# Odd-tile stores ahead of a K halo, two weight loads later, and residual accumulates moved into the next group's MLP1

## The chip, the cores and the metric

The kernel runs on one core of one Trainium2 chip. The metric is device time in microseconds (us), the median of several executions. In the text PE is TensorE (PEld its weight loads), DVE is VectorE, ACT is ScalarE, POOL is GpSimd and SP is SyncE, whose only work here is to issue DMAs.

## The reference

Input x is 2048 tokens of 576 numbers (bf16). Two blocks follow each other.

```python
xn = layernorm(x)
q, k, v = (xn @ wqkv)                    # 32 heads of 18
idx = pos - 2 * arange(8)                # token s looks at s, s-2, ..., s-14
attn = softmax(where(idx >= 0, q . k[idx] * 18**-0.5, -1e9))
h = x + (sum_w attn[w] * v[idx[w]]) @ wo
y = layernorm(layernorm(h))
out = h + gelu(y @ w1 + b1) @ w2 + b2    # w1: 576 x 4608, w2: 4608 x 576
```

## The kernel before, in words

**Tiles.** Token s = 16 p + j sits in partition p of tile j, so there are 16 tiles of 128 tokens. A token's eight neighbours are in the same partition of the tiles j, j-2, ..., and, where that runs below tile 0, in the partition above of a tile 16 higher. So K and V are kept in two rings (`kv_ring`, one of the even and one of the odd tiles), and when attention goes on from tile j to tile j-2, slot j is overwritten by its copy shifted by one partition. This is the **halo** (line 336 on): tile j's K and V are stored to DRAM (`store_halo`, L298) and read back one row lower (`kv_ring<-kv_dram`, L339), K (`halo(j, 1)`) and V (`halo(j, 2)`) by themselves. `halo(j, t)` can only be issued once DVE has read the slot for tile j, and the next tile's DVE work waits for its landing.

**Stages.** The first stage, QKV, has 24 visits of PE, each of two products (one of q, k or v of a tile). Even tiles come first and are transposed on PE. The odd tiles' normalised x goes through DRAM: ACT writes it (`ln1_act`), `out_x(i)` stores two tiles (L284 and L285, `xd<-q_all`), and `in_x(i)` reads them back transposed (L288, `xnT<-xd`). PE uses the first pair of odd tiles from visit 12 on. The lists `after` (what follows a visit) and `loads` (weight loads after a visit) order all that by hand. `load_w1(c)` reads one of six pieces of w1, and it waits for ACT's last evacuation before it.

Then there are eight **groups** of two tiles (GROUPS, counted from 0, even tiles first, both falling). For each group PE runs MLP1 (four visits, `pm`, L217), the output projection of the next group's two tiles (`pw<-wo_sb,oT`, L217) and MLP2 (`po`; L576 in groups 0 and 1; L664 from group 2 on, where seven products do the work of eight and DVE forms their sums, L634 and L644). A visit's second phase on PE waits for a marker, a no-operation on POOL that waits for the first phase (L227). Beside PE's work on group k:

- DVE finishes the attention of group k+1 in MLP1: for its first tile the weighted sum of V (L394, L400, L401), then the same for its second tile, which needs the V halo of the first; then the logits of group k+2 (L342 to L362).
- Each attention output is stored (`td<-q_all`, L193 and L194) and read back transposed (`oT<-td`, L430) for the output projection.
- Within MLP2, `ln2_h` (L458) adds the projection to x, giving h in float32; ACT computes the two layer norms, POOL the power -0.5 (L478); SP stores the result, and `ln2_in` (L493) reads it back transposed as `hnT`, the input of the next MLP1.
- **The residual.** `put_b2` (L502) overwrites the x tile with b2, and `accumulate_h` (L504 on) adds h to it by an accumulating DMA issued from POOL (`x_all<-h`, L505), behind the transposes of `ln2_in`. MLP2 of the next group reads the sum (L695).

`ln2_ins` (L873) issues the two transposes, and for all groups but the third and the last the two accumulates straight behind them, so in the MLP2 of the group before. The third group's (GROUPS[2]) are issued by L1018 ahead of visit 1 of its own MLP1. The last group takes another way (`add_b2`) and has no accumulate.

All engines' instructions are issued in the order in which the program calls them:

```python
ins = nc.gpsimd.dma_start(out=x_of(j), in_=h_of.pop(j)[:], accum_op=ALU.add).ins
tc.add_manual_dep(ins, read[0].name, sync_dep, reason="behind the transposes of LN2")
```

Of the kernel before, what the change touches and what calls it, by code (L numbers as in the profile page):

```python
# [17 lines left out]
def kernel(  # L18
# [37 lines left out]
    GROUPS = [ATT_ORDER[i:i + 2] for i in range(0, NT, 2)]  # L56
# [435 lines left out]
    def ln2_in(j):  # L492
        read[0] = nc.sync.dma_start_transpose(out=hnT_slot(j), in_=hn.pop(j)[:]).ins  # L493
        if stored[0] is not None:
            tc.add_manual_dep(read[0], stored[0].name, sync_dep, reason="stores ahead of the transposes of LN2")
            stored[0] = None
# [179 lines left out]
    def c_(fn, *a):  # L676
        return lambda: fn(*a)
# [69 lines left out]
    def call(fns):  # L747
        for fn in fns:
            fn()

    with tc.manual_schedule(engines={ENG.PE, ENG.Activation, ENG.DVE, ENG.SP, ENG.Pool}):
# [97 lines left out]
        A = ATT_ORDER  # L849
# [23 lines left out]
        def ln2_ins(c, d):  # L873
            for j in (c, d):
                ln2_in(j)
            if c not in (GROUPS[2][0], GROUPS[-1][0]):
                accumulate_hs(c, d)

        def accumulate_hs(*js):
            for j in js:  # L880
                accumulate_h(j)

        def ln2_pair(c, d):
            ln2_stats(c, d)
            ln2_send(c)
            ln2_send(d)
            ln2_ins(c, d)

        loads = {v: [c_(load_w1, c)] for c, v in enumerate((3, 4, 9, 13, 15, 17))}
        for n, v in enumerate((19, 20, 21, 22)):  # L890
            loads[v] = loads.get(v, []) + [c_(load_w2, n)]
        after = {
# [3 lines left out]
            3: [c_(ln1_even_rstd, 6, 7), c_(ln1_stats, 8)],  # L896
            4: [c_(ln1_rstd, 8), c_(ln1_stats, 9), c_(ln1_stats, 10, c_(ln1_bias, 8))],
            5: [c_(ln1_act, 8, 0), c_(ln1_rstd, 9), c_(ln1_bias, 9), c_(att_qk_a, A[0])],
            6: [c_(ln1_rstd, 10), c_(ln1_act, 8, 1), c_(halo, A[0], 1), c_(out_x, 0)],
            7: [c_(att_qk_rest, A[0], 0), c_(ln1_bias, 10), c_(ln1_act, 8, 2)],  # L900
            8: [c_(att_qk_a, A[1]), c_(att_qk_rest, A[1], 1), c_(ln1_act, 8, 3), c_(in_x, 0), c_(out_x, 1)],
            9: [c_(halo, A[1], 1), c_(ln1_act, 9, 0)],
# [49 lines left out]
        def mlp1_plan(p, q, r, s, end):  # L952
            return [[([2 * v + n], tag) for n, tag in enumerate(tags)] for v, tags in enumerate(((p, q), (r, s), (p, q), end))]

        def mlp1(grp, plan, ahead, between, late=None):
            for v, duos in enumerate(plan):
                call(ahead.get(v, ()))
                visit([mlp1_duo(grp, us, tag) for us, tag in duos], None, between.get(v, ()), late if v == 3 else None)

        def mlp2_tile(grp, i, tag, inserts):  # L960
            po_of[grp[i]] = psum_pair(tag, "po")
            mlp2(grp, i, [po_of[grp[i]][:, half, 0:HALF] for half in range(2)], inserts)
# [11 lines left out]
        def wo_visit(*duos, fill=False):  # L974
            visit([wo_duo(j, tag) for j, tag in duos], (lambda: [ahead[0]() for _ in range(2)]) if fill else None)
# [5 lines left out]
        for k, g in enumerate(GROUPS):  # L981
            c, d = GROUPS[k + 1] if k + 1 < len(GROUPS) else (None, None)
            e, f = GROUPS[k + 2] if k + 2 < len(GROUPS) else (None, None)
            m1, mid, ia, ib, late_wo = {0: []}, {}, {}, {}, None
            if k in (1, 2):
                m1[0].append(c_(finish_out, GROUPS[k - 1][1]))
            if k == 0:
                m1[0] += [c_(halos, 1), c_(load_w2, 4), c_(att_qk_a, d), c_(att_qk_rest, d, 1), c_(halo, d, 1)]
                mid[0] = {1: [c_(exps, d)]}
                m1[1] = [c_(pv_t, c), c_(pv_t, d), c_(att_qk_a, e), c_(halo, e, 1)]  # L990
                late_wo = wo_duo(c, "B")
                ia[0] = [c_(ln2_h, c), c_(ln2_act, c), c_(put_b2, c), c_(ln2_send, c), c_(att_qk_rest, e, 0)]
                ia[19] = [lambda d=d: wo_visit((d, "A"), fill=True), c_(ln2_h, d), c_(ln2_act, d), c_(put_b2, d), c_(att_qk_a, f),
                          c_(halos, 2), c_(halo, f, 1), c_(ln2_send, d), c_(ln2_ins, c, d), c_(att_qk_rest, f, 1), c_(exps, e, f)]
                ib[0] = [c_(finish_out, g[0]), c_(att_den, e, f), c_(pv_sum, e), c_(send_o, e)]
                ib[8] = [c_(read_o, e)]
            elif k == 1:
                m1[0] += [c_(pv_sum, d), c_(send_o, d)]
                m1[1] = [c_(att_qk_a, e), c_(halo, e, 1), c_(read_o, d), c_(att_qk_b, e, 0), c_(halos, 7)]
                m1[3] = [c_(att_qk_a, f), c_(halo, f, 1), c_(att_qk_add, f, ((0, 0, 9), (0, 0, 4)))]  # L1000
                ia[0] = [c_(wo_visit, (c, "B"), (d, "C")), c_(ln2_pair, c, d), c_(att_qk_b, f, 1, 2), c_(att_max, (e, f)),
                         c_(exps, e, f), c_(w2_sums, 0, 8, (0, 1)), c_(w2_sums, 8, 12, (0, 1)), c_(att_den, e, f)]
                ia[2] = [c_(pv_sum, e), c_(dma_tr_o, e), c_(reload_x, GROUPS[4])]
                ib[0] = [c_(finish_out, g[0])]
            if k < 2:
                mlp1(g, mlp1_plan(p, q, r, s, (s, r, p) if k else (r, s, p)), m1, mid, late_wo)
                mlp2_tile(g, 0, "D", ia)
                mlp2_tile(g, 1, "C", ib)
                continue
            rows = ROWS[k]  # L1010
            x = {n: [] for n in ("hc", "h", "6", "7", "in", "exp", "4", "3")}
            if 2 < k < 7:
                m1[0] += [c_(pv_sum, c), c_(send_o, c), c_(pv_sum, d), c_(read_o, c), c_(send_o, d), c_(read_o, d)]
            if k < 6:
                m1[1], m1[3] = [c_(att_qk_one, e, 0)], []
                if k == 2:
                    m1[0] += [c_(pv_sum, d), c_(send_o, d), c_(read_o, d)]
                    m1[1] = [c_(accumulate_hs, *g)] + m1[1]  # L1018
                    m1[3] += [c_(w2_sums, 0, 8, (2, 3)), c_(w2_sums, 8, 12, (2, 3)), c_(w2_sums, 12, 14, (0, 1)), c_(w2_sums, 14, 16, (0, 1)),
                              c_(att_qk_a, f), c_(halo, f, 1)]  # L1020
                early = {2: (), 5: (0,)}.get(k, (0, 2))
                m1[3] += [c_(h_sums, 0, min(rows, SR), early)]
                if k == 5:
                    x["h"] += [c_(h_sums, 0, SR, (2,)), c_(h_sums, 0, SR, (1, 3))]
                else:
                    x["h"] += [c_(h_sums, 0, rows, [t for t in range(4) if t not in early])]
                if k == 5:
                    x["h"] += [c_(h_sums, SR, rows), c_(w2_sums, 12, 14, (2, 3)), c_(w2_sums, 14, 16, (2, 3))]
                x["7"] += [c_(att_qk_one, f, 1) if k > 2 else c_(att_qk_b, f, 1), c_(att_max, (e, f))]
                x["exp"] += [c_(exps, e, f)]  # L1030
                x["4"] += [c_(att_den, e, f)]
            else:
                if k == 6:
                    ring1_free[0] = True
                    m1[1] = [c_(w2_sums, 16, NM)]
                m1[3] = [c_(h_sums, 0, SR)]
                if k == 7:
                    mid[3] = {1: [c_(h_sums, SR, 16)]}
                    x["h"] += [c_(h_sums, 16, NM)]
            if k + 3 < len(GROUPS):  # L1040
                x["in"] += [c_(reload_x, GROUPS[k + 3])]
            wo = None
            if c is not None:
                if k == 6:
                    x["hc"] += [c_(ln2_h, c), c_(ln2_act, c)]
                    x["h"] += [c_(ln2_h, d), c_(ln2_more, d), c_(ln2_rstd, d), c_(h_sums, SR, NM), c_(ln2_send, c),
                               c_(ln2_bias, d), c_(add_b2, c), c_(add_b2, d)]
                    x["6"] += [c_(ln2_hn, d), c_(ln2_out, d)]
                else:
                    x["hc"] = [c_(ln2_h, c), c_(ln2_act, c)] + x["hc"]  # L1050
                    x["h"] = [c_(ln2_h, d), c_(ln2_act, d), c_(put_b2, c), c_(put_b2, d)] + x["h"]
                    x["6"] += [c_(ln2_send, c)]
                    x["7"] = [c_(ln2_send, d)] + x["7"]
                x["in"] = [c_(ln2_ins, c, d)] + x["in"]
                wo = lambda tags: wo_visit((c, tags[0]), (d, tags[1]))
            mlp1(g, mlp1_plan(p, q, r, s, (r, s, p)), m1, mid)
            if 3 <= k < 7:
                mlp2_fast(g, rows, (s, p, q, r), wo, x, True)
                p, q, r, s = q, r, p, s
            else:  # L1060
                mlp2_fast(g, rows, (q, p, r, s), wo, x)
                p, q, r, s = r, s, p, q
# [30 lines left out]
```

## Time and profile before

| what | value |
|---|---|
| median of 5 runs | 363.87 us (363.86 to 364.19) |
| the profiled execution | 363.96 us |
| its span | 362.2 us |
| QKV and what precedes it | to 68.66 us |
| MLP1 of groups 0 to 7 starts at (us) | 68.66, 106.73, 144.47, 180.97, 217.28, 253.55, 289.52, 325.47 |
| one MLP1 on PE | 17.79 us |
| TensorE clock granted, mean | 0.998 |

The span is from the first to the last instruction of the program; the execution is longer by what lies around it. The starts of MLP1 come from the chain of waits, which goes back from the last instruction to whatever released it. "+2.97" in the text below is 2.97 us after the MLP1 of the group in question began. A number in square brackets in a timeline is the idle time of the engine before that instruction, and the name behind it is what ended it. The time "to landing" of a DMA runs from its issue on SP or POOL to the semaphore that tells of its arrival.

### The profile page before, as it was taken

Reading aid. Unit: us, or ns where it says so; the run is one execution under the profiler, and the core shown is the slowest. Engines: PE = TensorE matmul, PEld = TensorE weight load, DVE = VectorE, ACT = ScalarE, POOL = GpSimd, SP = SyncE. Lnnn points to the kernel's source line nnn. Section 1 sums busy time; section 2 is a strip of 40 time slices with the busy share of each in tenths; the row PEclk is TensorE's granted clock in tenths of the full one; section 3 lists DMA queues with packets and bytes.
Section 4 is the critical chain, followed back from the end, with each engine's and each line's share of the span. In section 5 each row is a group of like instructions: output and inputs, shape, how many; then the busy total and the mean of one; then the engine's idle time right before and its main releaser. Section 6 shows DMA issues by size and latency. Waiting matters only on the chain.

```text
span 362.2 us, 11410 instructions
## 1 busy us (share of the span) xinstructions
PE 357.4 (99%) x4891; PEld 291.3 (80%) x4891; DVE 302.1 (83%) x422; ACT 229.4 (63%) x507; POOL 37.1 (10%) x47
## 2 busy tenths in 40 slices
PE   8999999999999999999999999999999999999996
PEld 4688977888778877887788778877887788778874
DVE  5899999999999998999899989998899999720441
ACT  4779846798636782568556945695569366705630
POOL 2241004000120020101010210020101100100000
PEclk9999999999999999999999999999999999999999
DMA  8989899964446732621443144513541442120001
GB/s 232 317 213 283 226 253 235 355 239 74 149 88 110 193 139 71 131 61 51 120 89 90 50 123 85 91 49 88 120 78 60 60 84 74 39 54 19 2 2 33
DMA packets 61907, 43.70 MB, mean 121 GB/s; under 512 B 31888, under 2 KB 60176, under 8 KB 61856
## 3 DMA queue, kind: packets, MB, share of 16 engines
q1 hardware_dynamic: 59968, 41.13, 42.9%
q0 software_dynamic: 1728, 1.77, 4.6%
q8 instruction: 38, 0.62, 0.7%
q10 hardware_dynamic: 160, 0.07, 0.1%
q14 instruction: 13, 0.11, 0.1%
HBM read 21.10 MB, written 12.42 MB: 93 GB/s over the span
## 4 chain that ended last, share of the span: by engine, by line
PE 96%; DMA 2%; SPq 1%; issue 0%; DVE 0%
PE pm L217 39%; PE po L664 27%; PE pq L217 14%; PE po L576 10%; PE pw L217 5%; DMA wq_sb<-in_A_wqkv_dram 1%; SPq L104 1%; DMA oT<-td 1%; PE xt_pt L182 1%; PE o_pt L182 0%; PE h_pt L182 0%; PE xt_pt L186 0%; DVE o_sb L695 0%; PE o_pt L186 0%; PE h_pt L186 0%
## 5 line engine op out<-in xcount | busy, mean ns | idle before, releaser
L557 ACT ACTIVATE h_all<-pm,b_sb 128x256 f16<-128x256 f32 (+1 forms) x288 | 108.5, 497 | 69.6 <-PE pm L217 69.6
L217 PE MATMUL pm<-hnT,w_sb 64*128 64x256 bf16 x2304 | 143.0, 269 | 0.0
L217 PEld LDWEIGHTS <-w_sb 64*128 64x128 bf16 x2304 | 111.7, 94 | 15.1 <-issue 1.7
L664 PEld LDWEIGHTS <-h_all 128*128 128x128 f16 x512 | 49.4, 98 | 14.2 <-issue 1.6
L217 PE MATMUL pq<-wq_sb,xnT 64*128 64x288 bf16 x768 | 54.5, 283 | 0.3 <-DMA wq_sb<-in_A_wqkv_dram 0.3
L217 PEld LDWEIGHTS <-xnT 64*128 64x128 bf16 x864 | 42.7, 94 | 10.2 <-issue 0.5
L348 DVE TENSOR_TENSOR prod<-prod 128x2304 bf16<-128x2304 bf16 (+1 forms) x64 | 44.2, 691 | 2.0
L394 DVE TENSOR_TENSOR prod<-kv_ring,probs 128x4608 bf16<-128x4608 bf16 x16 | 40.9, 2555 | 2.4 <-DMA kv_ring<-kv_dram 2.2
L342 DVE TENSOR_TENSOR prod<-kv_ring,q_all 128x4608 bf16<-128x4608 bf16 x16 | 40.8, 2550 | 0.2
L217 PE MATMUL pm<-hnT,w1h_sb 64*128 64x256 bf16 x288 | 39.2, 269 | 0.0
L664 PE MATMUL po<-w2a_sb,h_all 128*128 128x288 bf16 (+1 forms) x282 | 38.9, 286 | 0.0
L400 DVE TENSOR_TENSOR prod<-prod 128x2304 bf16<-128x2304 bf16 (+1 forms) x32 | 33.9, 1058 | 1.1
L576 PEld LDWEIGHTS <-h_all 128*128 128x128 bf16 x288 | 27.9, 98 | 7.9 <-issue 1.0
L664 PEld LDWEIGHTS <-kv_ring 128*128 128x128 f16 x252 | 24.6, 98 | 6.3
L478 POOL TENSOR_TENSOR ln_rstd<-ln_var,mhalf 128x1 f32<-128x1 f32 x13 | 12.0, 924 | 170.1 <-ACT ln_var L477 170.1
L576 PE MATMUL po<-w2a_sb,h_all 128*128 128x288 bf16 x224 | 28.5, 286 | 0.0
L664 PE MATMUL po<-w2b_sb,h_all 128*128 128x288 bf16 (+1 forms) x142 | 21.3, 286 | 0.0
L217 PE MATMUL pw<-wo_sb,oT 64*128 64x288 bf16 x256 | 19.6, 283 | 0.2 <-DMA oT<-td 0.2
L735 ACT COPY po<-po 128x288 f32<-128x288 f32 x18 | 6.9, 384 | 19.6 <-PE po L664 18.5
L644 DVE TENSOR_TENSOR kv_ring<-h_all 128x1536 f16<-128x1536 f16 (+3 forms) x9 | 6.8, 752 | 14.7 <-ACT h_all L557 14.7
L162 POOL TENSOR_TENSOR ln_rstd<-ln_veps,mhalf 128x1 f32<-128x1 f32 (+2 forms) x14 | 13.4, 967 | 48.1 <-DVE ln_veps L156 32.9
L217 PEld LDWEIGHTS <-oT 64*128 64x128 bf16 x288 | 13.7, 94 | 4.6 <-issue 0.7
(110 smaller groups left out, 388.1 us busy)
## 6 DMA issues: line engine op xcount, KB each, us to landing
w_sb<-in_B_w_dram SPq DMA_DIRECT2D x6, 768.0 KB, 6.1
kv_ring<-kv_dram SPq DMA_DIRECT2D x28, 144.0 KB, 2.7
w2a_sb<-in_B_w_dram SPq DMA_DIRECT2D x4, 1008.0 KB, 6.6
kv_dram<-kv_ring SPq DMA_DIRECT2D x13, 288.0 KB, 3.0
out_dram<-o_sb SPq DMA_DIRECT2D x15, 144.0 KB, 2.6
td<-q_all SPq DMA_DIRECT2D x14, 144.0 KB, 1.8
td<-hn SPq DMA_DIRECT2D x14, 144.0 KB, 1.8
x_all<-in_A_x_dram SPq DMA_DIRECT2D x12, 144.0 KB, 2.8
```

Of the source, the lines that this page charges most:

```text
L162: nc.gpsimd.tensor_tensor(out=rstd[:], in0=veps[:], in1=mhalf[:].to_broadcast([P, n]), op=ALU.pow)
L217: last = nc.tensor.matmul(duo["g"][r ^ swap][i], lhsT=lhsT, rhs=rhs, start=(swap == 0 and i == 0 and kt == 0), stop=(swap == 1 and kt == K ...
L342: nc.vector.tensor_tensor(out=prod[:], in0=k_ring[j % 2], in1=q_all[:, j, :].unsqueeze(1) .to_broadcast([P, W, D]), op=ALU.mult)
L348: nc.vector.tensor_tensor(out=prod[:, :, o * H:o * H + n], in0=prod[:, :, a * H:a * H + n], in1=prod[:, :, c * H:c * H + n], op=ALU.add)
L394: nc.vector.tensor_tensor(out=prod[:].rearrange("p w (d h) -> p w d h", h=H), in0=v_ring[j % 2].rearrange("p w (d h) -> p w d h", h=H), in ...
L400: nc.vector.tensor_tensor(out=prod[:, 0:n, :], in0=prod[:, 0:n, :], in1=prod[:, n:2 * n, :], op=ALU.add)
L478: nc.gpsimd.tensor_tensor(out=rstd[:], in0=var[:], in1=mhalf[:], op=ALU.pow)
L557: pace[0] = nc.scalar.activation(out=hT(grp)[:, f, 0:N], in_=ps[:, r, i * N:(i + 1) * N], func=ACT.Gelu_apprx_tanh, bias=b1_sb[:, f:f + 1] ...
L576: nc.tensor.matmul(banks[half], lhsT=hT(grp)[:, f, i * P:(i + 1) * P], rhs=w2_rows(f)[:, half * HALF:(half + 1) * HALF], start=(f == 0), s ...
L644: nc.vector.tensor_tensor(out=s_slot(t, m0, m1), in0=a, in1=b, op=alu)
L664: nc.tensor.matmul(bank, lhsT=l, rhs=r, start=start, stop=stop, skip_group_check=True)
L735: nc.scalar.copy(out=bank[seed[step][1]], in_=bank[seed[step][0]])
```

## The change

There are three parts. `accumulate_hs` of GROUPS[3] to GROUPS[6] is no longer called in `ln2_ins` but ahead of visit 1 of the group's own MLP1, where GROUPS[2] has it already; GROUPS[1] stays as it was. After visit 6 of QKV the first store of odd tiles, `out_x(0)`, is issued ahead of the first K halo. The second piece of w1 is loaded after visit 8 instead of visit 4, and the third after visit 11 instead of visit 9.

```diff
         def ln2_ins(c, d):
             for j in (c, d):
                 ln2_in(j)
-            if c not in (GROUPS[2][0], GROUPS[-1][0]):
+            if c == GROUPS[1][0]:
                 accumulate_hs(c, d)
...
-        loads = {v: [c_(load_w1, c)] for c, v in enumerate((3, 4, 9, 13, 15, 17))}
+        loads = {v: [c_(load_w1, c)] for c, v in enumerate((3, 8, 11, 13, 15, 17))}
...
-            6: [c_(ln1_rstd, 10), c_(ln1_act, 8, 1), c_(halo, A[0], 1), c_(out_x, 0)],
+            6: [c_(ln1_rstd, 10), c_(ln1_act, 8, 1), c_(out_x, 0), c_(halo, A[0], 1)],
...
                 if k == 2:
                     m1[0] += [c_(pv_sum, d), c_(send_o, d), c_(read_o, d)]
-                    m1[1] = [c_(accumulate_hs, *g)] + m1[1]
...
+            if k < 7:
+                m1[1] = [c_(accumulate_hs, *g)] + m1[1]
             mlp1(g, mlp1_plan(p, q, r, s, (r, s, p)), m1, mid)
```

## The prediction

> **What bounds the kernel now.** I read the page first. Its first lines say that TensorE (PE) is busy for nearly the whole span, and the chain that ended last is 96% PE:
>
> ```profile
> span 362.2 us, 11410 instructions
> ...
> PE 357.4 (99%) x4891; PEld 291.3 (80%) x4891; DVE 302.1 (83%) x422; ACT 229.4 (63%) x507; POOL 37.1 (10%) x47
> ...
> PE 96%; DMA 2%; SPq 1%; issue 0%; DVE 0%
> ```
>
> The change adds and removes no matmul, so it can only move the places where PE waits. I looked for them twice: in the list of waits, and by the distance between the starts of neighbouring matmuls in the trace, less the usual distance of their kind (0.055 us in MLP1, 0.061 in QKV, 0.123 in MLP2). After the first 10 us only four distances are too long without being a change of stage: 0.17 us at 36.97 (two matmuls), 0.08 at 199.24, 0.17 at 275.33 and 0.46 at 307.64. Together **0.88 us**. The list of waits names their causes (PE and PEld rows describe the same stops, from two sides):
>
> ```profile
> DVE prod L394 <- DMA kv_ring<-kv_dram: 2.2, 3, 1.6
> ...
> PEld L217 <- DMA oT<-td: 0.7, 2, 0.5
> ...
> PEld L664 <- DVE h_all L644: 0.3, 1, 0.3
> ...
> PEld L217 <- DMA xnT<-xd: 0.2, 1, 0.2
> ```
>
> So 0.88 us is the most that can be won, 0.24% of the time: the transpose of the odd tiles (36.97), the attention output of group 4's second tile (199.24), a sum of h (275.33), and the attention output of group 7's second tile (307.64). A wait of DVE, 1.6 us, stands behind the last two.
>
> **Part 1, the accumulates of groups 3 to 6** (GROUPS counted from 0; group 7 has none). They leave four places and enter four. POOL's timeline shows the old places, and at 147.44 group 2's pair, which has the new place already:
>
> ```profile
> 147.44 1.79 POOL L505 DMA_DIRECT2D x_all<-h  x2 [13.62 <-PE pm L217]
> ...
> 180.22 1.78 POOL L505 DMA_DIRECT2D x_all<-h  x2 [9.09 <-DMA x_all<-in_A_x_dram]
> ...
> 215.90 1.78 POOL L505 DMA_DIRECT2D x_all<-h  x2 [8.19 <-DMA x_all<-in_A_x_dram]
> ...
> 253.58 1.78 POOL L505 DMA_DIRECT2D x_all<-h  x2 [9.59 <-DMA x_all<-in_A_x_dram]
> ...
> 288.48 1.78 POOL L505 DMA_DIRECT2D x_all<-h  x2 [9.18 <-DVE logits L362]
> ```
>
> Group 2's MLP1 starts at 144.47 (chain of waits), so the new place is +2.97 us into the MLP1; groups 3 to 6 start at 180.97, 217.28, 253.55 and 289.52, so their pairs go to about 183.9, 220.3, 256.5 and 292.5. Three things follow.
>
> POOL: behind the pair in the queue stand the markers of visit 1, which release PE's second phases. In group 2 the pair ends at +4.76, the next marker comes at +5.17 and PE has no gap. Cost 0, with 0.4 us of cover; the pair takes 1.78 to 1.79 us in all five rows above. Here a rule speaks against the change. The Trainium skill, "SBUF — State Buffer", section "SBUF: two separate sides", warns that a VectorE instruction in a two-port mode keeps GpSimd from writing DMA descriptors, 620 ns becoming 3100. By an estimate from these figures, five times 1.79 us would end the pair at +11.9 and hold PE 6.7 us in each of four groups, 27 us in all. The row at 147.44 ran beside the same L394 multiply that the new places meet and shows none of it; I go by the row.
>
> The old places: no PE wait is released by an accumulate there. What they delay is the V halo of the next group's first tile (L339), which DVE needs for the second weighted sum (L394):
>
> ```profile
> 187.15 2.56 DVE L394 TENSOR_TENSOR prod<-kv_ring,probs 128x4608 bf16<-128x4608 bf16 x1 [0.24 <-DMA kv_ring<-kv_dram]
> ...
> 261.06 2.56 DVE L394 TENSOR_TENSOR prod<-kv_ring,probs 128x4608 bf16<-128x4608 bf16 x1 [1.58 <-DMA kv_ring<-kv_dram]
> ```
>
> The halo is issued at +3.29 in groups 3, 4 and 5, as PE's end of the group before releases it, and lands 2.8, 2.3 and 4.1 us later. In group 4 the accumulates were nearly done, 2.3 us, no wait; in group 5 they had started only at 253.58. DVE is free for L394 at +5.94, so a halo has 2.65 us.
>
> The new places: all five pairs show their first packet 1.46 to 1.47 us after their start, so at +4.43. An undisturbed halo shows its first 0.94 us after its issue, +4.23, and lands at +5.5. It is ahead by 0.2 us. **Value taken: no wait of DVE in groups 3 to 5.** The other bound: one accumulate goes first; its packets take 1.4 us on each engine (255.0 to 256.4), so the halo lands at +6.9 and DVE waits 1.0 us. I take the first as group 4's row is nearest. The packets show stretches of one queue alone (255.0 to 256.4 POOL's, 256.1 to 257.0 SP's). The skill's "DMA: Bandwidth & Descriptors", section "Queues, rings and completion order", says that a DMA engine changes queues only between packets, drained whole; by it a halo ahead by 0.2 us loses nothing, one behind loses a whole share.
>
> What the freed DVE time is worth: in group 3 the attention output landed at 199.19, for a PE that wanted it at about 199.16; 0.24 us earlier removes the stop, **-0.08**. Group 4 has 1.6 us of slack (landing 233.93, use 235.54): 0. In group 5 the next thing late is not DVE: L458 waits for PE's output projection. It ran at 273.31, +19.76; in group 4, waiting for PE, at +19.54. So 1.58 us shrink to 0.22 there. From L458 on DVE has no gap until group 7's output is done (303.25), and its store and transpose (L193, L430) land at 308.12. All that comes 0.22 us earlier: the stop at 275.33 goes, the one at 307.64 stays, and the sum of both is **-0.22**.
>
> Group 6 is the doubtful one. DVE starts its sums there 2.5 us later than in the other groups (292.75, +3.23 against +0.71), so the halo goes out at 295.1, not before the accumulates but among them: pair at 292.5, first packet 293.95, last at +4.6 to +5.1 in the quiet rows, 297.1 to 297.6. It landed in 2.05 us before; DVE leaves it 2.68. An instruction fetch of 16 KB also takes one DMA engine from 294.64 for 1.15 us. Bounds: -0 and +0.95 us (that engine does the fetch, its share of 1.4 us until 297.9, then the halo, 298.75 landed). I take 0, near the landing of 2.8 us in group 3 with both kinds of traffic, and keep +0.95.
>
> **Part 2, out_x ahead of the K halo.** SP's timeline:
>
> ```profile
> 27.93 0.34 SPq L339 DMA_DIRECT2D kv_ring<-kv_dram  x1
> 28.36 0.39 SPq L284 DMA_DIRECT2D xd<-q_all  x1
> 28.80 1.55 SPq L285 DMA_DIRECT2D xd<-q_all  x1
> 30.44 1.96 SPq L298 DMA_DIRECT2D kv_dram<-kv_ring  x4
> 32.50 1.49 SPq L288 DMA_TRANSPOSE xnT<-xd  x1
> ```
>
> ACT ends the tile for out_x at 27.91 and DVE frees the halo's slot at 27.91 too, so out_x wins 0.4 us and the halo loses 0.9, or 2.4 if it is then the one that stays 1.5 us in the queue (a fetch runs from 28.88 to 29.96, and L285 sat through it). The halo landed at 31.33; DVE wants it at 32.33. So DVE loses 0 to 1.4 us. It has 1.2 us of cover: DVE's output ends at 46.20 and PE transposes it at 47.38. Value 0, worst 0.2. The gain: the transpose L288 landed at 37.09 for a PE that wanted it at 36.95. The stores L298 between set its issue; with out_x earlier it may come 0.4 us earlier or not at all. Bounds -0.17 and 0; I take **-0.1**.
>
> **Part 3, two w1 pieces later** (768 KB each, about 6 us to landing). They go from 23.34 to about 35.2 and from 35.74 to about 41.3, and are needed in MLP1 from 68.7 on: no wait. On SP's queue they now stand before the K halo of tile 12 (needed at 54.7) and before the V halo of tile 14 (landed 46.81, needed 47.59). The latter may come up to 1 us late, 0.2 after its slack; same cover. The second transpose landed at 42.83, use about 44.0: 1.1 us of slack, and one piece in flight beside it as before. Cost 0, worst +0.3.
>
> **Sum** against the profiled execution, 363.96 us (span 362.2 and 1.8 around it): -0.08 - 0.22 - 0.1 = -0.4, so 363.56. The median of the runs shown is 363.87, 0.09 lower, so about **363.5**.
>
> **Rivals.**
> Nothing lands where PE stands: group 5's halo is as late as before (its fetch at 258.72 still falls on it) and L288 does not move. 363.7 to 364.0, about 363.85. For it: DVE's 1.58 us are worth only 0.22. Against: group 4's quiet row.
> Group 6 alone collides: -0.08 - 0.22 - 0.1 + 0.95 = +0.55, 364.4.
> **Slower**: the accumulates win the DMA engines from the V halo. Place: L394's wait in the MLP1 of groups 3 and 6, where the attention output has no slack. Price: group 3 waits 1.0 instead of 0.24, +0.76; group 6 +0.95; less 0.1 at the start: +1.6, 365.5. It decides as soon as the pair's first packet comes before the halo's, 0.2 us from now. For it: the transpose in group 2 issued 0.8 us behind the pair took 4.8 us, against 2.9 elsewhere.
> Faster: all four stops go, also the oT of group 7, if its halo and transposes meet less traffic: -0.88, 363.0. Against: DVE's unbroken run from L458 on.
>
> **How the numbers follow.** Forecast (363.3 to 363.7) 0.38; nothing 0.22; group 6 alone 0.15; slower rival, 364.6 to 365.5, 0.13; faster rival 0.12. Keeping 8 in 10 leaves out the outer half of the slower rival and little else: 363.05 to 364.9. 0.2% is 0.73 us, about what a measurement of this kernel can tell from no change. Below 363.14 only the faster rival lies: 0.12. Above 364.6 the slower one: 0.13. The rest 0.75.
>
> **What would show it.** Right: L505 pairs at +2.97 of groups 2 to 6; L394 without a wait in groups 3 to 5; L458 of group 5 at +19.54 after a PE wait; a stop of about 0.4 us before group 7's oT; no xnT wait. Wrong: L394 waits of 0.5 us or more in group 3 or 6, a PE wait for oT near 199 or above 0.6 us near 308, or a PE wait for POOL's markers in visit 1, which I price at nothing.

## The result, and the profile after

The changed kernel takes 365.76 us (median of 43 runs, 364.34 to 367.81). The kernel before, run beside it on the same chip, takes 364.15 (79 runs). The ratio is 1.0039, with a 95% interval of 1.0031 to 1.0047. So the change makes the kernel **slower** by 1.4 us (1.1 to 1.7) by this ratio, well beyond the 0.2% that can be told from no change; the medians are 1.6 us apart. The forecast was 363.5.

The profiled execution after took 365.07 us, against 363.96 before. Its page, the same three lines that the prediction shows of before:

```profile
span 363.3 us, 11410 instructions
...
PE 357.1 (98%) x4891; PEld 291.1 (80%) x4891; DVE 302.2 (83%) x422; ACT 229.4 (63%) x507; POOL 37.1 (10%) x47
...
PE 94%; DMA 4%; SPq 1%; ACT 0%; issue 0%; DVE 0%
```

PE does the same work (357.1 us busy) in a span longer by 1.1 us. In the chain that ended last DMA has 4% where it had 2%. These are the lines of the chain in which PE waited for a transpose; the first of them, at 32.29, was not in the chain before:

```profile
32.29 5.06 DMA xnT<-xd
...
306.35 2.87 DMA oT<-td
```

The list of waits (us in total, times, longest) shows the same from PE's side:

```profile
PEld L217 <- DMA oT<-td: 1.7, 2, 1.4
...
DVE prod L394 <- DMA kv_ring<-kv_dram: 1.6, 3, 0.9
...
PE pw L217 <- DMA oT<-td: 1.1, 1, 1.1
...
PEld L217 <- DMA xnT<-xd: 0.5, 1, 0.5
...
PE pq L217 <- DMA xnT<-xd: 0.2, 1, 0.2
```

The wait for `oT` has grown from 0.5 to 1.4 us, and the wait for `xnT` from 0.2 to 0.5. By the distance between matmul starts, the stop near 37 is 0.40 us where it was 0.17 over two matmuls, the one near 199 is 0.20 (0.08 before), the one near 275 is gone (0.17), and the one near 308 is 1.37 (0.46).

A second measure separates the two halves of the change. Each profile is cut at its first QKV matmul and its first MLP1 matmul. QKV took 62.62 us after and 62.03 before (+0.59). From the first MLP1 matmul to the end it took 294.50 and 293.65 (+0.85). The first matmul itself came 0.33 us earlier. Together that is the 1.1 us of the span. The first of these numbers is the weaker: profiles of kernels with the QKV lists of before spread from 62.03 to 62.98 us.

**Group 6.** POOL's timeline shows the accumulates of groups 2 to 6, now all ahead of visit 1 and 1.78 us a pair as before:

```profile
147.70 1.79 POOL L505 DMA_DIRECT2D x_all<-h  x2 [13.65 <-PE pm L217]
...
184.27 1.78 POOL L505 DMA_DIRECT2D x_all<-h  x2 [12.88 <-PE pm L217]
...
220.60 1.78 POOL L505 DMA_DIRECT2D x_all<-h  x2 [12.50 <-PE pm L217]
...
256.90 1.78 POOL L505 DMA_DIRECT2D x_all<-h  x2 [12.53 <-PE pm L217]
...
292.75 1.78 POOL L505 DMA_DIRECT2D x_all<-h  x2 [13.25 <-DVE probs L390]
```

DVE's timeline, the multiply that needs the V halo, in groups 3, 4, 5 and 6:

```profile
187.21 2.56 DVE L394 TENSOR_TENSOR prod<-kv_ring,probs 128x4608 bf16<-128x4608 bf16 x1
...
223.63 2.56 DVE L394 TENSOR_TENSOR prod<-kv_ring,probs 128x4608 bf16<-128x4608 bf16 x1
...
259.96 2.56 DVE L394 TENSOR_TENSOR prod<-kv_ring,probs 128x4608 bf16<-128x4608 bf16 x1
...
299.03 2.56 DVE L394 TENSOR_TENSOR prod<-kv_ring,probs 128x4608 bf16<-128x4608 bf16 x1 [0.85 <-DMA kv_ring<-kv_dram]
```

There is no bracket in groups 3 to 5: in this profile DVE does not wait there any more (it waited 0.24 and 1.58 us before in groups 3 and 5). In group 6 it waits 0.85 us, where it did not wait before:

```profile
298.01 2.56 DVE L394 TENSOR_TENSOR prod<-kv_ring,probs 128x4608 bf16<-128x4608 bf16 x1
```

For group 5 one profile is not enough. All eight other profiles with that pair ahead of visit 1 show a wait there, of 0.35 to 0.81 us; the same kernel run again (f4_after, below) has

```profile
260.58 2.56 DVE L394 TENSOR_TENSOR prod<-kv_ring,probs 128x4608 bf16<-128x4608 bf16 x1 [0.53 <-DMA kv_ring<-kv_dram]
```

The DMA view of the changed kernel from 294.6 to 297.1 tells why group 6 waits:

```profile
DMA packets 250, 0.28 MB, mean 114 GB/s; under 512 B 16, under 2 KB 249, under 8 KB 249
...
q0 software_dynamic: 249, 0.27, 105.7%
q8 instruction: 1, 0.02, 2.4%
...
kv_ring<-kv_dram SPq DMA_DIRECT2D x1, 144.0 KB, 3.4
```

The V halo is issued in this stretch (at 295.53) and takes 3.4 us to landing, against 2.05 before. But of the 250 packets none is SP's: q0, POOL's queue with the accumulates, has the 16 engines for 2.5 us. The halo's first packet goes at 297.16, 1.63 us after its issue; undisturbed it goes 0.95 us after (before: 296.28). An instruction fetch of 16 KB (q8) starts at 295.58 and takes 0.98 us on its engine.

Up to 297.3 the last accumulate packets come close together; then five more follow one at a time, 0.19 us apart, until 298.26. That is what one engine that is 1 us behind the others would show, and the halo's own last packets end with it: fifteen of its 16 shares are done by 297.85, the last at 298.52 (the halo is 128 packets of 1152 bytes, and each share, one engine's part, ends with one of 4 bytes). The trace does not name the engine of a packet, so that it is the engine of the fetch is an inference. It is supported by the other profiles with the pair in this place: in e1, e4, f2 and f4 the last share is done 1.46 to 1.47 us after the end of a fetch, and 0.5 to 0.8 us after the fifteenth. In all five the fifteenth is done 0.16 to 0.34 us before DVE is free, and the landing is told 0.26 to 0.42 us after the last. So by an estimate from these figures DVE would have waited at most 0.2 us without the late share, instead of 0.71 to 0.85. No kernel here has the pair in this place without a fetch, so the two are not separated by a run.

From there the delay goes its way without loss: the second tile's store is issued at 304.30 instead of 303.28 and its transpose at 306.35 instead of 305.33. It lands at 309.22, and PE stands 1.37 us.

**QKV.** SP's timeline after (the same five lines of before stand in the prediction):

```profile
27.89 0.39 SPq L284 DMA_DIRECT2D xd<-q_all  x1
28.33 0.46 SPq L285 DMA_DIRECT2D xd<-q_all  x1
28.90 1.35 SPq L339 DMA_DIRECT2D kv_ring<-kv_dram  x1
30.34 1.85 SPq L298 DMA_DIRECT2D kv_dram<-kv_ring  x4
32.29 1.94 SPq L288 DMA_TRANSPOSE xnT<-xd  x1
```

The stores now go first, 0.47 us earlier, and the issue that stays over 1.3 us in SP's queue is the halo's (L339) instead of the second store's (L285). The transpose behind them is issued 0.21 us earlier but takes 1.94 us to issue instead of 1.49, and 5.06 us to landing instead of 4.59. It lands at 37.35, where it had landed at 37.09.

### The profile page after: what moved, and what is told of

Read it like the earlier page. It is cut to its first block, busy times and chain, and to the rows that moved or that the text cites. A ratio compares the mean times of both kernels' runs of the same rounds, so it can differ in the third digit from the quotient of the medians.

```text
span 363.3 us, 11410 instructions
## 1 busy us (share of the span) xinstructions
PE 357.1 (98%) x4891; PEld 291.1 (80%) x4891; DVE 302.2 (83%) x422; ACT 229.4 (63%) x507; POOL 37.1 (10%) x47
## 4 chain that ended last, share of the span: by engine, by line
PE 94%; DMA 4%; SPq 1%; ACT 0%; issue 0%; DVE 0%
PE pm L217 39%; PE po L664 26%; PE pq L217 12%; PE po L576 10%; PE pw L217 5%; DMA xnT<-xd 1%; DMA wq_sb<-in_A_wqkv_dram 1%; SPq L104 1%; DMA oT<-td 1%; PE xt_pt L182 1%; ACT kv_ring L312 0%; PE o_pt L182 0%; PE h_pt L182 0%; SPq L298 0%; PE xt_pt L186 0%
## 5 line engine op out<-in xcount | busy, mean ns | idle before, releaser
L394 DVE TENSOR_TENSOR prod<-kv_ring,probs 128x4608 bf16<-128x4608 bf16 x16 | 40.9, 2555 | 1.9 <-DMA kv_ring<-kv_dram 1.6
L505 POOL DMA_DIRECT2D x_all<-h x12 | 10.9, 1060 | 72.8 <-PE pm L217 51.6
```

Source lines behind the costliest of these rows:

```text
L394: nc.vector.tensor_tensor(out=prod[:].rearrange("p w (d h) -> p w d h", h=H), in0=v_ring[j % 2].rearrange("p w (d h) -> p w d h", h=H), in ...
```

## The experiments

Each ran beside the kernel before on the same chip: e1 to e4 on one, e5 to e8 on another, e9 to e12 on a third, f1 to f4 on a fourth. "+" is the difference of the medians; the interval is that of the ratio, in which a thousandth is 0.36 us. Two stretches of each profile serve as a finer measure: "QKV" from the first QKV matmul to the first MLP1 matmul (62.03 us before), and "the rest" from there to the end (293.65 before).

| kernel | what it has | + us | ratio, 95% | QKV | rest |
|---|---|---|---|---|---|
| e1_acc | part 1 | +0.58 | 1.0024 (0.9998 to 1.0049) | 62.13 | 294.64 |
| e2_qkv | parts 2 and 3 | +2.07 | 1.0048 (1.0023 to 1.0074) | 63.98 | 294.26 |
| e3_acc345 | groups 3 to 5 | -0.05 | 0.9991 (0.9970 to 1.0011) | 62.37 | 293.61 |
| e4_acc6 | group 6 | +0.71 | 1.0008 (0.9984 to 1.0033) | 62.98 | 294.76 |
| e5_swap | part 2 | +0.18 | 0.9995 (0.9968 to 1.0021) | 62.70 | 293.74 |
| e6_w1 | part 3 | +0.80 | 1.0014 (0.9993 to 1.0035) | 62.45 | 293.96 |
| e7_acc_v2 | groups 3 to 6, ahead of visit 2 | +0.99 | 1.0020 (1.0005 to 1.0035) | 62.38 | 294.46 |
| e8_acc_6v2 | groups 3 to 5 visit 1, 6 visit 2 | +0.06 | 1.0002 (0.9984 to 1.0019) | 62.66 | 293.86 |
| e9_w12 | part 2, w1 (3, 8, 12) | +0.31 | 1.0005 (0.9997 to 1.0014) | 62.43 | 293.65 |
| e10_third | part 2, w1 (3, 4, 11) | +0.58 | 1.0020 (1.0009 to 1.0030) | 63.09 | 293.87 |
| e11_second | part 2, w1 (3, 8, 9) | +1.19 | 1.0032 (1.0018 to 1.0047) | 64.42 | 293.93 |
| e12_6v2_w12 | e8 and e9 together | +0.69 | 1.0016 (1.0004 to 1.0027) | 61.78 | 294.38 |
| f1_no6 | the change without group 6 | +0.40 | 1.0011 (0.9999 to 1.0023) | 62.74 | 293.74 |
| f2_noswap | the change without part 2 | +1.42 | 1.0027 (1.0011 to 1.0044) | 62.67 | 294.61 |
| f3_345_w12 | groups 3 to 5, w1 (3, 8, 12) | -0.11 | 0.9995 (0.9986 to 1.0005) | 61.77 | 293.66 |
| f4_after | the change | +1.36 | 1.0033 (1.0020 to 1.0046) | 62.16 | 294.51 |

### The halves: part 1 alone, parts 2 and 3 alone

e1_acc takes over only the accumulates of groups 3 to 6; the lists of QKV are those of before.

```diff
-            if c not in (GROUPS[2][0], GROUPS[-1][0]):
+            if c not in (GROUPS[2][0], GROUPS[3][0], GROUPS[4][0], GROUPS[5][0], GROUPS[6][0], GROUPS[-1][0]):
...
+            if k in (3, 4, 5, 6, 2):
+                m1[1] = [c_(accumulate_hs, *g)] + m1.get(1, [])
```

> Part 1 alone: the accumulates of GROUPS[3] to [6] ahead of visit 1 of their own MLP1, QKV as before. Theory A (collision in group 6: the V halo goes out among the packets of the accumulates and DVE's second weighted sum waits for it): L394 waits 0.6 to 1.0 us near 298, PE stands 1.2 to 1.5 us near 308, and the time is 0.5 to 1.0 us above the kernel before. Theory B (the loss is made in QKV, by the later K halo and the later weight pieces): the time is 0 to 0.4 us below the kernel before.

e2_qkv takes over only the two lists.

```diff
-        loads = ... enumerate((3, 4, 9, 13, 15, 17))}
+        loads = ... enumerate((3, 8, 11, 13, 15, 17))}
...
-            6: [..., c_(halo, A[0], 1), c_(out_x, 0)],
+            6: [..., c_(out_x, 0), c_(halo, A[0], 1)],
```

> Parts 2 and 3 alone: out_x(0) ahead of the first K halo and two w1 pieces later, accumulates as before. Theory A: within 0.4 us of the kernel before, a stop of 0 to 0.5 us at the first use of the odd tiles near 37 and the stop near 308 at 0.4 to 0.6 us as before. Theory B: 0.7 to 1.5 us above the kernel before, with PE waits in QKV or in group 0 that make up that sum.

Part 1 alone shows the stop near 308 at 1.36 us, as in the changed kernel, and none near 37. Parts 2 and 3 alone show the stop near 37 (0.85 us), a new one of 1.0 us near 55, and the one near 308 at 0.52, about as before. So both halves cost something, and in the profiles the cost of part 1 sits where the profile after has it, that of parts 2 and 3 near 37 and, new, near 55. Parts 2 and 3 cost more than either theory had (1.5 us at most). The sum of the medians (+2.65) is more than the whole; f1 to f4, below, take that up.

### Which groups: 3 to 5, or 6

e3_acc345 moves groups 3 to 5 and leaves group 6; e4_acc6 moves group 6 alone. Both edit the condition in `ln2_ins` and the set of `k`.

```diff
+            if k in (3, 4, 5, 2):        # e3; e4: (6, 2)
+                m1[1] = [c_(accumulate_hs, *g)] + m1.get(1, [])
```

> Only the accumulates of GROUPS[3] to [5] are moved, GROUPS[6] stays in the MLP2 of group 5, QKV as before. Theory A: no collision is left, so 0.2 to 0.5 us below the kernel before; no wait of L394 in groups 3 to 5, the stop near 275 gone, the stop near 308 at 0.2 to 0.5 us. Theory B: the same sign, 0 to 0.4 us below. A third theory (every moved pair disturbs the halos of its group): at or above the kernel before.

> Only the accumulates of GROUPS[6] are moved, the rest as before. Theory A: the whole loss in one move, 0.7 to 1.2 us above the kernel before, L394 waiting 0.6 us or more near 298 and PE 1.1 us or more near 308. Theory B: within 0.2 us of the kernel before.

e3: the stops near 199 and 275 are gone, the one near 308 is 0.53 us, and the time is that of before. DVE still waits 0.55 us in group 5, where the expectation had no wait, and the gain of 0.2 to 0.5 us that it named does not show. e4: DVE waits in group 6 (0.71 us), the stop near 308 is 1.27 us, and the rest is 1.1 us longer. Its median is +0.71, but the interval of its ratio holds 1. The rest tells it better, over all the kernels of this study. With groups 3 to 5 moved, it is 294.50 to 294.64 us where group 6 is in visit 1 too (after, e1, f2, f4; mean 294.57) and 293.61 to 293.74 where group 6 is in MLP2 (e3, f1, f3; mean 293.67): **0.9 us** apart. With groups 3 to 5 in MLP2, it is 294.76 (e4) against 293.65 to 294.26 (before, e2, e5, e6, e9, e10, e11; mean 293.87): again 0.9. The same rows give groups 3 to 5 a gain of 0.2 us (293.87 less 293.67), within the spread of single profiles.

### Can group 6 go later? Visit 2

e7_acc_v2 puts the pairs of groups 3 to 6 ahead of visit 2, e8_acc_6v2 only group 6's.

```diff
+            if k == 6:                   # e8; e7: k in (3, 4, 5, 6)
+                m1[2] = [c_(accumulate_hs, *g)] + m1.get(2, [])
```

> The accumulates of GROUPS[3] to [6] ahead of visit 2 instead of visit 1 (3.9 us later), QKV as before. If the loss of group 6 is the collision of the packets with the V halo issued at about +6.0 (theory A), the pair's first packet at about +8.4 is behind it, L394 waits nowhere in groups 3 to 6, the stop near 308 is 0.3 to 0.6 us, and the time is 0.2 to 0.5 us below the kernel before. If it is the accumulates in MLP1 as such (any place there delays the transposes of the attention output), 0.5 us or more above, with stops for oT near 199 and 308.

> Part 1 with one difference: GROUPS[6]'s accumulates ahead of visit 2, those of GROUPS[3] to [5] ahead of visit 1; QKV as before. Theory A: as with GROUPS[6] left in MLP2, 0 to 0.5 us below the kernel before, no L394 wait near 298, the stop near 308 at 0.3 to 0.6 us. Otherwise as part 1 alone, 0.5 us above.

POOL issues group 6's pair at 296.62 in e8, 7.0 us into the MLP1 instead of 3.0, behind the halo. DVE's multiply does not wait:

```profile
298.14 2.56 DVE L394 TENSOR_TENSOR prod<-kv_ring,probs 128x4608 bf16<-128x4608 bf16 x1
```

But now the store of the first attention output meets the accumulates. SP's timeline of e8, then of the changed kernel (the two stores, then the transpose that waits for their landing):

```profile
298.13 0.34 SPq L193 DMA_DIRECT2D td<-q_all  x1
298.51 0.45 SPq L194 DMA_DIRECT2D td<-q_all  x1
302.05 1.42 SPq L430 DMA_TRANSPOSE oT<-td  x1
```

```profile
298.21 0.34 SPq L193 DMA_DIRECT2D td<-q_all  x1
298.59 0.43 SPq L194 DMA_DIRECT2D td<-q_all  x1
300.23 1.21 SPq L430 DMA_TRANSPOSE oT<-td  x1
```

The transpose comes 3.9 us after the store instead of 2.0, and pushes the second tile's store and transpose behind it. The stop near 308 is 0.75 us in e8 and 1.10 in e7, and the rest is 293.86 and 294.46 us, so 0.2 and 0.8 of the 0.9 us remain. The collision is exchanged for another one, less costly in e8's profile and hardly less in e7's. Neither visit 1 nor visit 2 is a free place for group 6's pair.

### Parts 2 and 3, one at a time

> Part 2 alone: out_x(0) ahead of the first K halo, the rest as before. If the swap costs (theory B1: the halo and the four K/V stores behind it move nothing forward, and the transpose of the first odd pair lands later), PE stops 0.3 to 0.9 us at the first use of the odd tiles near 37 and the time is 0.2 to 0.7 us above the kernel before. If the later w1 pieces are what costs (theory B2), it is within 0.2 us of the kernel before.

> Part 3 alone: the second and third w1 piece after visits 8 and 11. Theory B2: the third piece, issued straight ahead of the V halo of tile 14, holds that halo back; it takes 4.3 to 6.2 us to landing instead of 3.3, DVE's L394 near 48 waits 0.5 to 2.2 us, PE stands 0.5 to 1.2 us near 54 for the transpose of tile 12's attention output; 0.5 to 1.5 us above the kernel before. Theory B1: within 0.3 us.

e5: L288 is issued at 32.25 and lands at 37.13, and the stop near 37 is 0.16 us, about as before. The swap by itself brings nothing that can be told, and a cost or a gain below about 1 us would not show in this interval. e6: the V halo of tile 14 takes 4.5 us where it took 3.3, DVE waits 0.52 us for it, PE does not stop near 55; the median is +0.80, and the interval holds 1.

### Which of the w1 pieces

All three have part 2. e9_w12 issues the third piece after visit 12, behind the V halo; e10_third moves only the third piece, e11_second only the second.

```diff
-        loads = ... enumerate((3, 4, 9, 13, 15, 17))}
+        loads = ... enumerate((3, 8, 12, 13, 15, 17))}     # e9
+        loads = ... enumerate((3, 4, 11, 13, 15, 17))}     # e10
+        loads = ... enumerate((3, 8, 9, 13, 15, 17))}      # e11
```

> Parts 2 and 3, but the third w1 piece after visit 12, so behind the V halo of tile 14 on SP's queue. Theory B2 (the piece straight ahead of the V halo is what costs): the halo lands 3.1 to 3.7 us after its issue, no L394 wait near 48, no long stop near 55; what is left is the stop at the odd tiles' first use, and the time is 0 to 0.5 us above the kernel before, 1 us or more below parts 2 and 3. If the loss is the swap's or that of the pieces anywhere else: 1.5 us above or more.

> Parts 2 and 3 with the second w1 piece left after visit 4: the swap and the third piece after visit 11. Theory B2: the V halo takes 4.3 to 6.2 us to landing, L394 waits near 48, 0.8 to 2 us above the kernel before, as parts 2 and 3. Otherwise 0 to 0.4 us above.

> Parts 2 and 3 with the third w1 piece left after visit 9: the swap and the second piece after visit 8. Theory B2: the V halo as before (3.1 to 3.7 us), 0 to 0.5 us above the kernel before. If the second piece, straight behind out_x(1), is what delays the stores of the odd tiles: a later second transpose (landed after 43.5), a PE stop near 44, 0.5 us or more above.

e9: the V halo takes 2.9 us, there is no wait on it and no stop near 55. e10: the piece is issued at 42.81, 1.1 us ahead of the halo; the halo takes 5.8 us, DVE waits 1.85 for it, and PE stops 0.6 us near 55; the median, +0.58, is below the 0.8 to 2 us expected. e11: two pieces stand together ahead of the second transpose:

```profile
36.11 0.52 SPq L104 DMA_DIRECT2D w_sb<-in_B_w_dram  x1
36.74 0.50 SPq L339 DMA_DIRECT2D kv_ring<-kv_dram  x1
37.34 0.44 SPq L104 DMA_DIRECT2D w_sb<-in_B_w_dram  x1
40.42 1.86 SPq L288 DMA_TRANSPOSE xnT<-xd  x1
```

This transpose is issued 1.7 us later than before (38.71) and lands 5.4 us after its issue; PE stops 1.22 us near 44.6. So either piece is cheap where it stands behind the DMA that is next needed, and costs a stop where it stands ahead of it.

### Both mends together

e12_6v2_w12 is the changed kernel with group 6 in visit 2 and the third piece after visit 12.

> The changed kernel with both mends: GROUPS[6]'s accumulates ahead of visit 2 and the third w1 piece after visit 12; groups 3 to 5 and the swap as in the change. Theories A and B2 together: 0 to 0.5 us above the kernel before at most, 1.1 to 1.6 us below the changed kernel, V halo 3.1 to 3.7 us, no L394 wait near 48 or 298, the stop near 308 at 0.3 to 0.8 us. If something else in the change costs: 0.8 us or more above the kernel before.

QKV is 61.78 us, with no wait near 55, but the stop near 308 is 0.98 us. It is still slower than before (+0.69), more than the 0 to 0.5 us expected, and the stop that is left is group 6's.

### What the whole is made of, on one chip

f1_no6 is the change with group 6 back in MLP2, f2_noswap the change with the stores behind the halo again, f3_345_w12 has groups 3 to 5 and the third piece after visit 12, without the swap. f4_after is the changed kernel.

> The changed kernel, with the accumulates of group 6 alone left in MLP2 of group 5, where they were. Theory A (group 6's accumulates hold up its V halo, and the stores' swap with the later w1 pieces delays the odd transposes): no L394 wait near 298, a stop of PE near 308 of 0.3 to 0.6 us instead of 1.37, a stop near 37 of 0.2 to 0.8 us as in the changed kernel; median 0.4 to 0.9 us below that of the changed kernel in this call, still 0.5 to 1.2 above before. Theory B (the swap and the pieces carry all of it, and group 6's loss is made up elsewhere): within 0.3 us of the changed kernel.

> The changed kernel, with the odd tiles' stores behind the first K halo again, as they were; accumulates of groups 3 to 6 and w1 pieces as changed. Theory A: no stop of PE on xnT near 37 above 0.2 us, the V halo of tile 14 takes about 4.4 us to land but its lateness is mostly covered, group 6's stop near 308 stays at 1.2 to 1.5 us; median 0.4 to 1.0 us above before, 0.3 to 0.8 below the changed kernel. Theory B (the swap costs nothing by itself): the same as the changed kernel within 0.3 us.

> The accumulates of groups 3 to 5 in visit 1, group 6's left in MLP2, the stores as before, and the third w1 piece after visit 12 instead of 11, behind the V halo. Theory A: V halo of tile 14 lands in 3.0 to 3.7 us, no stop near 37 or 55, a stop near 308 of 0.3 to 0.5 us; median from 0.4 below to 0.2 above before. Theory B (any delay of w1 costs): 0.3 to 0.8 above before.

> The changed kernel itself, beside the three above on one chip. Both theories: 1.1 to 1.9 us above before; stops of PE near 37 (0.2 to 0.8 us) and near 308 (1.2 to 1.5 us).

f4 gives +1.36 us and f1 +0.40, so **group 6 is worth 0.96 us** by the medians (0.8 by the ratios, 1.0033 less 1.0011), in line with the 0.9 us of the rest. DVE's multiply in group 6, in f4 and then in f1:

```profile
299.22 2.56 DVE L394 TENSOR_TENSOR prod<-kv_ring,probs 128x4608 bf16<-128x4608 bf16 x1 [0.84 <-DMA kv_ring<-kv_dram]
```

```profile
299.06 2.56 DVE L394 TENSOR_TENSOR prod<-kv_ring,probs 128x4608 bf16<-128x4608 bf16 x1
```

f2 did not do what my theory said: without the swap the time is the same as with it (+1.42 and +1.36). The stop near 37 is on average longer with the swap: in the nine profiles with it, its longest distance is 0.15 to 0.85 us too long (mean 0.44; e5, which has the swap alone, 0.16), in the nine without it 0 to 0.23. But between f2 and f4 this makes no difference in time; in f2's profile the stop near 55 is the larger for it (0.99 against 0.19 us). That one stop is given back at the other is a guess from these two profiles, no more. What f1, f2 and f4 share is the third w1 piece ahead of the V halo. SP's timeline of f1, the piece and the halo:

```profile
41.61 0.45 SPq L104 DMA_DIRECT2D w_sb<-in_B_w_dram  x1
43.38 0.34 SPq L339 DMA_DIRECT2D kv_ring<-kv_dram  x1
```

DVE's timeline of f1, and PE's, where the transposes of the next attention output wait for DVE's L458 behind that multiply:

```profile
49.52 2.56 DVE L394 TENSOR_TENSOR prod<-kv_ring,probs 128x4608 bf16<-128x4608 bf16 x1 [2.06 <-DMA kv_ring<-kv_dram]
```

```profile
55.48 0.44 PE L182 MATMUL o_pt<-ident,q_all 128*128 128x128 bf16 x5 [0.87 <-DVE h L458]
```

The piece (768 KB) lands at 47.56 and the halo behind it in the same queue at 49.42, 6.0 us after its issue. In f3 the order is the other way round, and the multiply does not wait:

```profile
43.05 0.34 SPq L339 DMA_DIRECT2D kv_ring<-kv_dram  x1
43.43 0.43 SPq L104 DMA_DIRECT2D w_sb<-in_B_w_dram  x1
```

```profile
47.16 2.56 DVE L394 TENSOR_TENSOR prod<-kv_ring,probs 128x4608 bf16<-128x4608 bf16 x1
```

Over all profiles with the piece ahead, the halo takes 4.4 (after), 4.5 (e6), 5.3 (f4), 5.8 (e10), 6.0 (f1), 6.2 (e2) and 6.3 us (f2); DVE's wait is 0.36, 0.52, 1.32, 1.85, 2.06, 2.23 and 2.28 in the same order; and the stop near 55, the distance less its usual 0.215, is 0, 0, 0.19, 0.56, 0.94, 0.97 and 0.99. Where there is a stop, it is the wait less 1.1 to 1.3 us. With the piece behind (e9, e12, f3) the halo takes 2.9, 3.3 and 3.8 us, and there is neither wait nor stop.

The fetches count here too. In 14 of the 18 profiles (all but e2, e3, e4 and e11) the last share of this halo is done 0.81 to 0.84 us after the end of a fetch of 16 KB. With the piece ahead that fetch starts at 45.5 to 47.4 us, without it at 43.9 to 44.8. So in six of these seven profiles how late the halo is behind a piece goes with when the fetch ran; why the fetch runs later there is not shown.

f3 takes 364.21 against 364.32 (0.9995, 0.9986 to 1.0005). It is the changed kernel without the swap and its two losses, and it is the same as the kernel before (-0.5 to +0.2 us by the interval). No version that was run is faster than before.

## Why the prediction was wrong

**What bounds the kernel.** Right. PE's stops were the place to look, and two of the four named grew; that a new one could open, near 55, was priced too low. The 0.88 us was rightly called the most that could be won; the choice of -0.4 was then made of three small gains against losses put at 0.

**POOL's markers, 0.** Right. No wait of PE for a marker is in the list after, and the pairs take 1.78 us in all the new places, beside DVE's multiplies. The 27 us, the estimate by the rule of the Trainium skill on VectorE and GpSimd ("SBUF — State Buffer", section "SBUF: two separate sides"), are not there. The same section says that `tensor_tensor`, the operation of L394, has no two-port mode, so the rule did not speak against this change; the prediction missed that and was kept right by its row.

**Groups 3 to 5, no wait of DVE.** Right for groups 3 and 4, half right for group 5, wrong in the size of what it brings. In the profile after, the halos land in 2.3, 2.3 and 2.6 us, all before the multiply, and in all nine profiles with these pairs ahead of visit 1 the halo's first packet goes 0.5 to 0.8 us before the pair's. But in eight of the nine DVE waits 0.35 to 0.81 us in group 5, so the clean profile was luck. There the last share is done 0.81 to 0.90 us after the end of a fetch in all nine, as in e7 (0.90), whose wait of 0.27 us has no accumulate near it. That is the mechanism of the rival "nothing lands where PE stands", which named the fetch at 258.72. L458 of group 5 runs at +19.55 of its MLP1 after a wait for PE; the prediction had +19.54. But the 0.3 us that this should have brought are not to be told from nothing: 0.2 by the means of the rest above, 0.05 and 0.11 by the medians of e3 and f3. The two stops read from one profile were partly that execution's own. Near 199 the stop is 0.15 to 0.48 us in the profile after, e1, e8, e12, f1 and f2, where the accumulates of group 3 have moved, and nothing in e3, f3 and f4, which have them in the same place; near 275 there is none in e5, e9, e10 and e11, where group 5's have not moved.

**Group 6, "bounds -0 and +0.95, I take 0".** This is the main step that failed. The working of the upper bound was what happened, almost to the number: the halo behind the pair's packets, one engine late by a fetch, landing at 298.75. It landed at 298.94, DVE waited 0.85 us, and the kernel lost 0.8 to 1.0 (the fetch came at 295.58, not at 294.64). The choice went wrong by its reference row: 2.8 us in group 3 was a halo issued after the accumulates had mostly gone, in another order of the two transfers. The row at hand was the prediction's own sentence on groups 3 to 5, that 0.2 us decide there who goes first. Group 6's halo is issued 2.8 us after the pair and so is behind it by any reading.

A page bears on this. The Trainium skill, "DMA: Bandwidth & Descriptors", section "Queues, rings and completion order", says that an engine goes round its queues packet by packet and drains a whole packet of descriptors before it changes; the prediction read it as "one behind loses a whole share". What the profile counts as a packet is one row of 1152 bytes, eight to an engine for each of these transfers. Most of the traces agree: 248 of the pair's 256 rows had gone before the halo's first one, and on the late engine of e1, e4, f2 and f4 the pair's rows run out before the halo's eight follow in one block. The changed kernel's own profile does not: on its late engine rows of the pair and of the halo alternate one by one from 297.4 to 298.4. Either way the halo is done last. The prediction applied its reading to groups 3 to 5, where it helped, and not to group 6, where it spoke against the change.

**Part 2, "-0.1".** No gain came of it, and the sign of its small effect is not told. The stores were issued 0.47 us earlier (27.89 for 28.36), about as forecast, but the slow issue of 1.3 to 1.5 us fell on the halo instead of the second store, and the four halo stores (L298), issued at 30.34 where it had been 30.44, set the transpose's issue as feared. The stop that it was to shorten is longer in most kernels with the swap, not shorter. In time it makes no difference in f2 against f4, and costs 0.4 us in e9 (with the swap, +0.31) against f3 (without it but with groups 3 to 5 moved, -0.11, on another chip).

**Part 3, "cost 0, worst +0.3".** Failed in its worst case. The prediction let the V halo be up to 1 us late and had a cover of 1.2 us. Measured, the halo behind a piece lands 0.4 to 2.3 us too late for DVE: fifteen of its 16 shares are done at about the time when the piece of 768 KB lands (by 47.06 in f1, where it lands at 47.56), and the last one, in six of the seven profiles, 0.8 us after a fetch. The cover of 1.2 us was right in size, though it is not the output at 46.20 that has it but the next one, near 55. What was wrong is the lateness. The loss is 0 to 1.0 us from one profile to the next; by the timed runs it is 0.3 to 0.6 us (e10 less e9: 0.27 by medians, 0.5 by ratios; f1 less f3, which differ in the swap too: 0.5 and 0.6), with intervals about as wide as the difference.

**The sum.** -0.4 was taken. Measured: 0 to -0.2 from groups 3 to 5, +0.9 from group 6, about +0.5 from parts 2 and 3 together, in sum +1.2 to +1.4; the timed runs gave 1.4 (1.1 to 1.7) and in f4 1.2 by the ratio. The rival "group 6 alone" had the mechanism and gave 364.4; it got 0.15, too little. The slower rival's price of 365.5 is close to the result, but half of its mechanism is not there (group 3 does not wait) and the w1 piece ahead of the V halo took its place, so that price is right by luck.

**What stays open.** e2_qkv, parts 2 and 3 alone, took +2.07 us, while f1, which has the same two and groups 3 to 5, took +0.40 on another chip. The stops explain their profiles (63.98 and 62.74 us of QKV), not why the same lists run so differently there. In kernels with the QKV part of before, single profiles of QKV spread from 62.03 to 62.98 us, so effects below 0.5 us in this stage are told only by the timed runs. Why the first odd transpose takes longer to issue after the swap (1.94 against 1.49 us) was not found. What the accumulates of group 6 would cost without the fetch was only estimated.

## What to carry to other kernels

When a DMA is moved, ask for every transfer that is issued in the 3 us behind it, on its own queue and on others, who is served first: the one that is behind pays, here 1.4 us behind two accumulates of 144 KB and 1 to 3 us behind a load of 768 KB. A transfer has landed only when the last of its 16 shares has, and beside an instruction fetch one share came 0.5 to 1.5 us later than the rest (group 6 of five kernels; tile 14 of the eight without a piece ahead), so keep that much cover beside what the queue costs. A bound that was worked out by a mechanism and a neighbour's row that knows nothing of the mechanism are not equal evidence; take the bound when the order of issue is already known. And a kernel whose tensor engine stops for 0.9 us in 362 has little to win by reordering, while each of its uncovered transfers can lose that much.

## What the runs showed of the hardware

- **Long issues on SP go with instruction fetches.** Before, L285 took 1.55 us to issue at 28.80; after, in the same place, L339 took 1.35 us at 28.90 (a fetch of 16 KB runs from 28.54 for 1.31 us); in e2 L285 took 1.83. Usual is 0.33 to 0.5 us. It falls on whichever DMA is there. Over all 18 profiles, from 15 us on and without the stores of L298, 108 of the 115 plain DMA issues of SP that took over 1 us overlap a fetch; but so do 216 that took under 0.6 us, so a fetch does not always do it.
- **An accumulating DMA is slow.** Its packets took 0.17 us each against 0.05 for the halo's, both of 1152 bytes. The halo issued 2.8 us behind a pair sent its first packet 1.60 to 1.64 us after its issue (after, e1, e4, f2, f4) instead of 0.95.
- **A fetch of 16 KB makes one share of a transfer late.** Beside a fetch the V halo's last share is done 0.81 to 0.84 us after the end of the fetch (tile 14, 14 profiles), 0.81 to 0.90 in group 5 (ten), and 1.46 to 1.47 behind a pair of accumulates (group 6; e1, e4, f2, f4).
- **A halo of 144 KB behind a load of 768 KB on SP's queue** took 4.4 to 6.3 us to landing, ahead of it 2.9 to 3.8.
